# A transformer block in fp32 on one core: attention scores of two or four heads through one bank and one Exp, and other due times for projections

## The chip, the core and the metric

The kernel runs on one core of one Trainium2 chip. The metric is the device time of one execution in microseconds. PE is TensorE (the weight loads have a row of their own, PEld), DVE is VectorE, ACT is ScalarE, POOL is GpSimd, and SP is the engine that issues nearly all DMAs.

## The reference

One pre-norm transformer block over 2048 tokens of width 448: layer norm, attention with 16 heads of 28 in a sliding window of 256 tokens, a residual, layer norm, a gated GELU feed-forward of width 1792, and a residual. All in float32.

```python
def _A_ref(x, wqkv, wo):
    B, S, D = x.shape
    H = 16; Dh = D // H; W = 256
    qkv = (lambda x, *d: x.transpose(*d))((x @ wqkv).reshape(B, S, 3, H, Dh), 2, 0, 3, 1, 4)
    q, k, v = qkv[0], qkv[1], qkv[2]
    scores = jnp.einsum("bhqd,bhkd->bhqk", q, k) * (Dh ** -0.5)
    idx = jnp.arange(S)
    mask = (idx[:, None] - idx[None, :] >= 0) & (idx[:, None] - idx[None, :] < W)
    scores = jnp.where(mask[None, None], scores, -1e9)
    p = _softmax(scores, axis=-1)
    o = jnp.einsum("bhqk,bhkd->bhqd", p, v)
    return (lambda x, *d: x.transpose(*d))(o, 0, 2, 1, 3).reshape(B, S, D) @ wo
...
x = A_x
h = x + _A_ref(_layernorm(x, axis=-1), A_wqkv, A_wo)
h2 = h + _B_ref(_layernorm(h, axis=-1), B_w_gate, B_w_up, B_w_down)
```

`_B_ref` is `(gelu(x @ w_gate) * (x @ w_up)) @ w_down`.

## The kernel before, in words

**Tiling.** The 2048 tokens are 16 tiles of 128, in 4 chunks `c` of 4 tiles. The 16 heads are 4 groups `g` of 4 heads. A *block* `B = 4c + g` is the attention of one chunk for one group of heads, 16 blocks in all. To keep float32 accuracy on TensorE, an operand is kept as a high part and a low part (`to_hi` on ACT, L349; `to_lo`, the difference, mostly on DVE, L352), and a product is a sum of several matmuls (`TERMS`, 11 per projection tile).

**Stages of a chunk.** Layer norm (`ln1`), then the projections `project` to q and k (L622: 7 tiles of 11 matmuls a chunk, 128x512 each; their parts go out to DRAM through SP, L632 and L634), and `values` (L570). `loads` brings q and k back, laid out by head (`rq`, `rk`, L654).

**Stages of a block.** `scores` (L672) gives query-by-key scores, of which DVE takes the row maxima (L676). `maxima` puts the maxima, split in two parts, into extra rows of `rq` (L703 on TensorE, then two ACT copies), so that a second product of `rk` and `rq` yields key-by-query scores with the maximum already subtracted. `probs` does that second product (L744) and the Exp on ACT (L748), for each of the six key tiles `m` that a chunk's four query tiles can see. Key tile `m` has the query tiles `parts(m)`: one for m = 0 and 5, two for m = 1 and 4, three for m = 2 and 3. The first chunk has only m = 2 to 5. Before, `probs` is called once for each of the 4 heads `j`: one matmul of 128, 256 or 384 columns into a bank of its own, one Exp out of it. `select` masks the edges on POOL (L759) for all four heads together, `attend` multiplies by the values (L778) in two halves of three key tiles, `drain` transposes and divides by the sum, and after every second group `output` applies the output weights (L835) and adds to the residual `hres`.

**Feed-forward.** 56 products of a chunk and 128 of the inner columns. The first four use full-height matmuls (L1008) and are partly done while attention still runs; all later ones run as pairs of half-height matmuls (L984). Their order on TensorE is written out in `feed_forward`. Weights come from DRAM (`weight_load`) and are split (`weight_splits`).

**What sets the order.** Every operation is put into a list with its engine, a cost, a latency and a *key*, a due time. `Lists.run` then goes through a model of the engines: at each step an engine takes, among the operations that could start first (within an ease of some hundredths of a microsecond), the one with the smallest key. The resulting order is the order of each engine's instructions. So a key or a cost changes the order of instructions, and all engines then run their queues in that order, waiting for one another by semaphores. The 8 banks of TensorE's output are handed out in that pass too: `allowed` gives banks 2 and 3 to `prob` (and 7 once the projections are issued), 0 and 1 to `score`, 4 and 5 to the attention sums, 6 and 7 to projections, values and outputs.

**Names that the change touches.** `EDGE` is how far ahead of a block the projections are due (`base`, L618), `LN1` and `LN2` are due times of layer norms, `LEAD` that of the second layer norm of the last two chunks against the feed-forward, `VKEY` that of the values, `FETCH` that of a DRAM-to-DRAM copy of the third weights (L896). A block is 16 units of key long. `WKEY` in the changed kernel replaces the expression `16 * NB + 5 * loaded` with `NB = 16` and `loaded` 0 and 1.

Of the kernel before, what the change touches and what calls it, by code (L numbers as in the profile page):

```python
# [11 lines left out]
AF = mybir.ActivationFunctionType  # L12
# [9 lines left out]
SCALE = float(DH) ** -0.5  # L22
# [5 lines left out]
NB = NG * CS  # L28
# [4 lines left out]


LAG_T = 6
LAG_P = 15
LAG_V = 12
EDGE = 9
WIN = 14
FFN = 1000  # L40
LEAD = 30
MARGIN = 0.7
START = 0.8
EARLY = 2
# [1 line left out]
HOLDO = 1  # L46
AHEAD = 7
BEHIND = 5
LN1 = (0, -19, 55, 134)
LN2 = (166, 224)  # L50
VKEY = (-30, -23, 14, 24)
VHALF = 0
FETCH = 170
PKS = 3
POOLED = (3,)
PKX = (2, 3)
# [12 lines left out]
def mm(n):  # L69
    return max(n / 2400 + 0.0155, 0.115)  # L70
# [156 lines left out]
def block_kernel(ctx: ExitStack, tc, x, wqk_in, wv_in, wo_in, ffn_in, out):  # L227
    nc = tc.nc
# [332 lines left out]
               [WVRAW(p, b), WV(p, 0, b)], [WV(p, 1, b)], port=True)  # L561

    def values(t, p, n):
        key = 64 * (t // 4) + VKEY[t % 4] if t > 3 else 8 * t - 37 if not p else VHALF + 6 * t
        b = Bank("v")
        w = slice(224 * p, 224 * (p + n))
        c = slice(128 * col(t), 128 * col(t) + 128)
        for a in range(NP):
            h, wb, xb = TERMS[a]
            op("pe", mm(224 * n), 0.29 if n == 1 else 0.38, key + a / 16, lambda a=a, h=h, wb=wb, xb=xb: nc.tensor.matmul(  # L570
                bank[b.k][:, 0:224 * n], xT[:, xb, c], wv[:, h, wb, w], start=(a == 0),
                stop=(a == NP - 1)), [XT(col(t)), *(WV(p + i, h, wb) for i in range(n))], () if a else [V(t, p, n)], b, tag="v")
        op("act", 0.29 if n == 1 else 0.47, 0.39 if n == 1 else 0.57, key + 1, lambda: to_hi(
            v[:, at_v(t), 8 * p:8 * (p + n), 0:DH], bank[b.k][:, 0:224 * n].rearrange("p (h d) -> p h d", d=DH)),
           ["ones"], [V(t, p, n)], b)
# [35 lines left out]
    def project_tile(c, m):  # L611
        g, s = divmod(m, 2)
        cc = 12 * (c % 2)
        hl, both, tok = pk_at()
        B = 4 * c + g
        b = Bank("proj")
        per = 1 if m == 6 else 2
        base = 16 * B - EDGE  # L618
        for a in range(NP):
            h, wb, xb = TERMS[a]  # L620
            key = -33 + 6 * m + a / 4 if B < 2 else base - WIN * (1 - (s * NP + a) / (per * NP))
            op("pe", mm(512) + 0.002, 0.403, key, lambda a=a, h=h, wb=wb, xb=xb: nc.tensor.matmul(  # L622
                bank[b.k], wqk[m][:, h, wb, :], xT[:, xb, cc * 128:cc * 128 + 512], start=(a == 0),
                stop=(a == NP - 1)), [span("xT", cc, 4), WQK(m, h)], (), b, tag="proj")
# [106 lines left out]
    def pp_at(o, n, j=None):  # L731
        return [span("pp", 4 * (o + i) + (j or 0), 4 if j is None else 1) for i in range(n)]

    ORDER = {0: 0, 1: 1.3, 2: 4, 3: 8, 4: 12, 5: 14.6}

    def probs(B, m, j, o):
        u = B % 2
        lo, hi = parts(m)
        n = (hi - lo + 1) * 128
        b = Bank("prob")  # L740
        key = 16 * B + LAG_P + ORDER[m] + j * n / 384

        def one():
            nc.tensor.matmul(bank[b.k][:, 0:n], rk[u][0:104, j, m * 128:m * 128 + 128],  # L744
                             rq[u][0:104, j, lo * 128:(hi + 1) * 128], start=True, stop=True)

        def exp():
            nc.scalar.activation(pp[:, j, o * 128:o * 128 + n], bank[b.k][:, 0:n], AF.Exp, scale=SCALE)  # L748
        q = [("rk", u, m), *(("pick", u, j) for j in range(4)), *((w, u, i) for i in range(lo, hi + 1) for w in ("rq", "rx"))]
        op("pe", mm(n), 0.19 + n / 2400, key, one, q, (), b, tag="prob")  # L750
        op("act", 0.065 + n * 0.00088, 0.16 + n * 0.00088, key, exp, (), pp_at(o, hi - lo + 1, j), b, tag="exp")

    def select(B, m, o):
        lo, hi = parts(m)
# [177 lines left out]
    def feed_forward():  # L932
        first = [4 * sum(GROUPS[:gi]) + k for gi, gn in enumerate(GROUPS) for k in range(gn)]
        loaded = split = -1
        n = 0
        for gi, gn in enumerate(GROUPS):
            for c in range(4):
                down = [Bank(("down", i)) for i in range(4)]
                for k in range(gn):
                    i = sum(GROUPS[:gi]) + k  # L940
                    while loaded < 2:
                        loaded += 1
                        split += 1
                        weights(loaded, 16 * NB + 5 * loaded if loaded < 2 else FFN + 30 * first[loaded] - 20)
                    if n == PAIRED:
                        for cc in (1, 2, 3, 0):
                            cs = slice(512 * cc, 512 * cc + 512)
                            dma(FFN + 30 * PAIRED - 25 + cc, 128, lambda cs=cs: nc.sync.dma_start(
                                f(rec[2][64:128, cs]), f(xT[0:64, 3, cs])), [span("xT", 4 * cc, 4), "fp"], [("xh", cc)])
                    product(n, i, c, k, gn, gi, down)  # L950
                    while split < NF - 1 and first[split + 1] <= n + BEHIND:
                        split += 1
                        weight_splits(split, FFN + 30 * first[split] - 20, phase[n][0][0:1])
                    while loaded < NF - 1 and first[loaded + 1] <= n + AHEAD:
                        loaded += 1
# [168 lines left out]
    for c in range(CS):  # L1124
        project(c)
        if c == 0:
            clear()
            for t in range(4):
                values(t, 1, 1)
        else:  # L1130
            values(4 * c + 2, 0, 2)
            values(4 * c + 3, 0, 2)
        if c == 3:
            free("wqkfree", ["proj"])
            free("wvfree", ["v"])
            ln2(0)
        for g in range(NG):
            B = 4 * c + g
            loads(B)
            if B in (1, 2):  # L1140
                wo_weights(2 * B - 2)
                wo_weights(2 * B - 1)
            for i in range(4):
                for j in range(4):
                    scores(B, i, j)
                if i % 2:
                    maxima(B, i // 2)
            at = slots(B)
            for half in ((0, 1, 2), (3, 4, 5)) if c else ((2, 3), (4, 5)):
                for m in half:  # L1150
                    for j in range(4):
                        probs(B, m, j, at[m])
                    select(B, m, at[m])
                attend(B, half, at)
            drain(B)
            if g % 2:
                output(g // 2, c)
            if g == 0 and c < 3:
                ln1(c + 1)
# [106 lines left out]
```

## Time and profile before

| | |
|---|---|
| time, median of 3 runs | 727.81 us (727.71 to 727.92) |
| time of the profiled execution | 727.88 us |
| its span | 726.2 us |
| instructions | 15085 |
| DMA | 82.06 MB, mean 113 GB/s |

Times in the profile count from the start of the span. A row of a group has the line, the engine, the operation, output and inputs with their shapes, the count, then busy time in us and the mean of one in ns, and last the idle time of the engine just before these instructions and what ended it. A matmul's end in the profile is modelled, so how fast TensorE goes is read from the starts of matmuls that follow each other.

### The profile page before, as it was taken

The numbers are of one execution on the slowest core, as the hardware profiler recorded it, in microseconds if no ns is written. First come the engines' busy times: TensorE is split into PE (matmuls) and PEld (weight loads), VectorE is DVE, ScalarE is ACT, GpSimd is POOL, SyncE is SP. The second block draws the span as 40 slices with busy tenths as digits, with TensorE's granted clock in tenths as the row PEclk, the third lists the DMA queues.
The fourth block names the chain that finished last, engine by engine and source line by source line (L and its number), as shares of the span: only waits on it lengthen the run. The fifth ranks groups of instructions, "written<-read, shape, count | busy, mean of one in ns | idle before, by whom it ended". The sixth has DMA issues, their size and how long they took to land.

```text
span 726.2 us, 15085 instructions
## 1 busy us (share of the span) xinstructions
PE 717.8 (99%) x5732; PEld 594.4 (82%) x5732; DVE 401.4 (55%) x1067; ACT 366.4 (50%) x927; POOL 162.6 (22%) x285
## 2 busy tenths in 40 slices
PE   8999999999999999999999999999999999999997
PEld 7887778878787877778888888888888888888886
DVE  7968779978787769658464313244133234232224
ACT  7738777777867787786453222244222223222221
POOL 5504743544354446741000000000000000000000
PEclk9999999999999999999999999999999999999999
DMA  8896867888548984342732000012100000001002
GB/s 308 268 311 211 234 159 203 214 255 207 161 122 241 242 234 136 77 112 42 203 105 84 1 2 1 1 44 83 42 1 2 1 1 1 2 1 51 19 34 102
DMA packets 96929, 82.06 MB, mean 113 GB/s; under 512 B 41736, under 2 KB 83016, under 8 KB 96840
## 3 DMA queue, kind: packets, MB, share of 16 engines
q1 hardware_dynamic: 96712, 80.98, 38.5%
q8 instruction: 45, 0.74, 0.4%
q14 instruction: 28, 0.23, 0.1%
q10 hardware_dynamic: 144, 0.11, 0.0%
HBM read 50.27 MB, written 31.03 MB: 112 GB/s over the span
## 4 chain that ended last, share of the span: by engine, by line
PE 94%; DVE 2%; ACT 1%; issue 1%; DMA 1%; POOL 0%; SPq 0%; DVEq 0%; POOLq 0%
PE bank L984 53%; PE bank L622 10%; PE bank L744 6%; PE bank L672 6%; PE bank L778 5%; PE bank L570 5%; PE bank L835 5%; PE bank L1008 3%; DMA hres<-in_x_dram 1%; PE bank L404 1%; DVE mt L676 1%; PE bank L703 0%; ACT pp L748 0%; DVE hres L1086 0%; ACT xT L349 0%
## 5 line engine op out<-in xcount | busy, mean ns | idle before, releaser
L676 DVE CUSTOM_DVE_ANT_0 mt<-bank,mt 128x384 bf16<-128x384 f32 (+2 forms) x256 | 126.8, 526 | 29.0 <-PE bank L672 27.2
L748 ACT ACTIVATE pp<-bank 128x384 f32<-128x384 f32 (+2 forms) x352 | 122.5, 388 | 39.8 <-PE bank L744 36.8
L1050 DVE TENSOR_TENSOR mt<-bank,mt 128x512 f32<-128x512 f32 x54 | 37.1, 688 | 143.3 <-ACT mt L1048 143.3
L759 POOL TENSOR_SCALAR_AFFINE_SELECT pp<-pp 128x512 f32<-128x512 f32 x120 | 75.9, 646 | 107.6 <-ACT pp L748 86.3
L744 PE MATMUL bank<-rq,rk 104*128 104x384 f32 (+2 forms) x352 | 97.6, 303 | 0.6 <-ACT pp L748 0.2
L622 PE MATMUL bank<-xT 128*128 128x512 f32 x308 | 94.9, 400 | 0.0
L1048 ACT ACTIVATE mt<-bank 128x512 f32<-128x512 f32 x54 | 32.2, 596 | 118.0 <-PE bank L984 118.0
L984 PE MATMUL bank<-xT,rk 64*128 64x512 f32 x656 | 82.0, 388 | 0.0
L984 PE MATMUL bank<-xT,rec 64*128 64x512 f32 x656 | 81.9, 388 | 0.0
L672 PE MATMUL bank<-rk,rq 84*128 84x384 f32 (+2 forms) x256 | 80.8, 346 | 0.8 <-DVE mx L676 0.5
L744 PEld LDWEIGHTS bank<-rq,rk 104*128 104x128 f32 x352 | 65.0, 189 | 17.4 <-ACT pp L748 5.9
L984 PEld LDWEIGHTS bank<-xT,rk 64*128 64x128 f32 x656 | 63.0, 184 | 12.2
L984 PEld LDWEIGHTS bank<-xT,rec 64*128 64x128 f32 x656 | 63.0, 184 | 12.1
L1086 DVE TENSOR_TENSOR hres<-bank,hres 128x448 f32<-128x448 f32 (+1 forms) x65 | 35.7, 611 | 66.9 <-PE bank L984 64.8
L990 ACT ACTIVATE e<-bank 1x1 f32<-1x1 f32 x162 | 25.7, 158 | 81.2 <-PE bank L984 80.5
L984 PE MATMUL bank<-xT,proj 64*128 64x512 f32 x533 | 66.6, 388 | 0.0
L622 PEld LDWEIGHTS bank<-xT 128*128 128x128 f32 x308 | 55.4, 189 | 7.4 <-ACT v L349 0.4
L984 PEld LDWEIGHTS bank<-xT,proj 64*128 64x128 f32 x533 | 51.1, 184 | 9.9
L672 PEld LDWEIGHTS bank<-rk,rq 84*128 84x128 f32 x256 | 46.3, 189 | 12.2 <-DVE mx L676 5.2
L570 PE MATMUL bank<-proj,xT 128*128 128x448 f32 (+1 forms) x220 | 51.0, 337 | 0.2 <-ACT v L349 0.2
L778 PE MATMUL bank<-pp,v 128*29 128x384 f32 (+2 forms) x704 | 45.4, 388 | 0.0
L349 ACT ACTIVATE rq<-bank 8x512 fp32r<-8x512 f32 x64 | 37.5, 586 | 13.6 <-PE bank L703 12.6
(147 smaller groups left out, 1088.5 us busy)
## 6 DMA issues: line engine op xcount, KB each, us to landing
rk<-k SPq DMA_DIRECT2D x44, 336.0 KB
rq<-q SPq DMA_DIRECT2D x32, 336.0 KB
v<-in_ffn_dram SPq DMA_DIRECT2D x7, 736.0 KB
q<-proj SPq DMA_DIRECT2D x11, 448.0 KB
raw<-in_ffn_dram SPq DMA_DIRECT2D x6, 736.0 KB
xn<-xn SPq DMA_DIRECT2D x72, 56.0 KB
xT<-xn SPq DMA_DIRECT2D x20, 192.0 KB
hres<-in_x_dram SPq DMA_DIRECT2D x16, 224.0 KB
```

The costliest lines, as they stand in the source:

```text
L349: nc.scalar.activation(dst, src, AF.Copy)
L570: op("pe", mm(224 * n), 0.29 if n == 1 else 0.38, key + a / 16, lambda a=a, h=h, wb=wb, xb=xb: nc.tensor.matmul(bank[b.k][:, 0:224 * n], x ...
L622: op("pe", mm(512) + 0.002, 0.403, key, lambda a=a, h=h, wb=wb, xb=xb: nc.tensor.matmul(bank[b.k], wqk[m][:, h, wb, :], xT[:, xb, cc * 128 ...
L672: nc.tensor.matmul(bank[b.k][:, o:384], rq[u][0:3 * DH, j, i * 128:i * 128 + 128], rk[u][0:3 * DH, j, m0 * 128:(i + 3) * 128], start=True, ...
L676: nc.vector.tensor_tensor_reduce(junk[s % 2][:, o:384], bank[b.k][:, o:384], mask[:, o:384], 1.0, -BIG, OP.add, OP.max, mx[i // 2][:, i % ...
L744: nc.tensor.matmul(bank[b.k][:, 0:n], rk[u][0:104, j, m * 128:m * 128 + 128], rq[u][0:104, j, lo * 128:(hi + 1) * 128], start=True, stop=True)
L748: nc.scalar.activation(pp[:, j, o * 128:o * 128 + n], bank[b.k][:, 0:n], AF.Exp, scale=SCALE)
L759: nc.gpsimd.affine_select(a, a, pattern=[[0, 4], [-cm, 128]], compare_op=op_, fill=0.0, base=0, channel_multiplier=cm)
L778: nc.tensor.matmul(bank[b.k][32 * j:32 * j + DH + 1, lo * 128:(hi + 1) * 128], v[:, at_v(4 * c - 2 + m), 4 * g + j, :], pp[:, j, at[m] * 1 ...
L835: op("pe", mm(D), 0.38, wk, lambda a=a, h=h, oh=oh, wh=wh, i=i, k=k: nc.tensor.matmul(bank[k.k][:, 0:D], ohl[:, h, oh, i * 128:(i + 1) * 1 ...
L984: nc.tensor.matmul(bank[bk.k][:, 0:n], w, m, start=bool(start), stop=bool(stop), tile_position=(64 * x, 0), skip_group_check=True)
L1050: op("dve", 0.605, 0.702, key + 2 * NP, lambda: nc.vector.tensor_tensor(blocks(g2), src(1), blocks(g2), op=OP.mult), [*G2, *held[1]], G2, ...
```

## The change

`probs` is called once for a key tile instead of once for each head. It puts `G = 512 // n` heads into one bank: four heads where a key tile has one query tile (n = 128), two where it has two (n = 256), one where it has three (n = 384). One Exp then reads the whole bank and writes `G` strided pieces. The planner's cost for the matmuls is a new formula. The due times named above get other values; for the last chunk the projections are due 4 units earlier (`ELAST`), and its second value tile 2 units earlier (`VLAST`).

```diff
+VLAST = (-30, -25, 14, 24)
+ELAST = 4
+WKEY = (256, 261)
...
-EDGE = 9
+EDGE = 8
...
-LEAD = 30
+LEAD = 10
...
-LN1 = (0, -19, 55, 134)
-LN2 = (166, 224)
+LN1 = (0, -19, 55, 128)
+LN2 = (166, 231)
...
-FETCH = 170
+FETCH = 210
...
-        key = 64 * (t // 4) + VKEY[t % 4] if t > 3 else 8 * t - 37 if not p else VHALF + 6 * t
+        key = 64 * (t // 4) + (VKEY if t < 12 else VLAST)[t % 4] if t > 3 else 8 * t - 37 if not p else VHALF + 6 * t
...
-        base = 16 * B - EDGE
+        base = 16 * B - EDGE - (ELAST if c == 3 else 0)
...
-    def probs(B, m, j, o):
+    def probs(B, m, o):
         u = B % 2
         lo, hi = parts(m)
         n = (hi - lo + 1) * 128
-        b = Bank("prob")
-        key = 16 * B + LAG_P + ORDER[m] + j * n / 384
-
-        def one():
-            nc.tensor.matmul(bank[b.k][:, 0:n], rk[u][0:104, j, m * 128:m * 128 + 128],
-                             rq[u][0:104, j, lo * 128:(hi + 1) * 128], start=True, stop=True)
-
-        def exp():
-            nc.scalar.activation(pp[:, j, o * 128:o * 128 + n], bank[b.k][:, 0:n], AF.Exp, scale=SCALE)
...
-        op("pe", mm(n), 0.19 + n / 2400, key, one, q, (), b, tag="prob")
-        op("act", 0.065 + n * 0.00088, 0.16 + n * 0.00088, key, exp, (), pp_at(o, hi - lo + 1, j), b, tag="exp")
+        G = 512 // n
+        for j in range(0, 4, G):
+            b = Bank("prob")
+            key = 16 * B + LAG_P + ORDER[m] + j * n / 384
+
+            def some(j=j, b=b):
+                for i in range(G):
+                    nc.tensor.matmul(bank[b.k][:, n * i:n * i + n], rk[u][0:104, j + i, m * 128:m * 128 + 128],
+                                     rq[u][0:104, j + i, lo * 128:(hi + 1) * 128], start=True, stop=True)
+
+            def exp(j=j, b=b):
+                nc.scalar.activation(pp[:, j:j + G, o * 128:o * 128 + n],
+                                     bank[b.k][:, 0:G * n].rearrange("p (g t) -> p g t", g=G), AF.Exp, scale=SCALE)
...
+            cost = G * (n / 2400 + 0.009)
+            op("pe", cost, cost + 0.17, key, some, q, (), b, tag="prob")
+            op("act", 0.065 + G * n * 0.00088, 0.16 + G * n * 0.00088, key, exp, (),
+               [p for i in range(G) for p in pp_at(o, hi - lo + 1, j + i)], b, tag="exp")
...
-                        weights(loaded, 16 * NB + 5 * loaded if loaded < 2 else FFN + 30 * first[loaded] - 20)
+                        weights(loaded, WKEY[loaded] if loaded < 2 else FFN + 30 * first[loaded] - 20)
...
-                    for j in range(4):
-                        probs(B, m, j, at[m])
+                    probs(B, m, at[m])
```

The planner's cost of one matmul, `mm(n)`, is `max(n / 2400 + 0.0155, 0.115)` us; it stays in use for all other matmuls.

More of the change, by code (lines that the diff above doesn't have):

```diff
@@ L739, in probs @@
         n = (hi - lo + 1) * 128
-        b = Bank("prob")
-        key = 16 * B + LAG_P + ORDER[m] + j * n / 384
-        def one():
-            nc.tensor.matmul(bank[b.k][:, 0:n], rk[u][0:104, j, m * 128:m * 128 + 128],
-                             rq[u][0:104, j, lo * 128:(hi + 1) * 128], start=True, stop=True)
-        def exp():
-            nc.scalar.activation(pp[:, j, o * 128:o * 128 + n], bank[b.k][:, 0:n], AF.Exp, scale=SCALE)
-        q = [("rk", u, m), *(("pick", u, j) for j in range(4)), *((w, u, i) for i in range(lo, hi + 1) for w in ("rq", "rx"))]
-        op("pe", mm(n), 0.19 + n / 2400, key, one, q, (), b, tag="prob")
-        op("act", 0.065 + n * 0.00088, 0.16 + n * 0.00088, key, exp, (), pp_at(o, hi - lo + 1, j), b, tag="exp")
+        G = 512 // n
[9 more added lines that the diff above has]
+                                     bank[b.k][:, 0:G * n].rearrange("p (g t) -> p g t", g=G), AF.Exp, scale=SCALE)
+            q = [("rk", u, m), *(("pick", u, i) for i in range(4)),
+                 *((w, u, i) for i in range(lo, hi + 1) for w in ("rq", "rx"))]
+            cost = G * (n / 2400 + 0.009)
+            op("pe", cost, cost + 0.17, key, some, q, (), b, tag="prob")
+            op("act", 0.065 + G * n * 0.00088, 0.16 + G * n * 0.00088, key, exp, (),
+               [p for i in range(G) for p in pp_at(o, hi - lo + 1, j + i)], b, tag="exp")
     def select(B, m, o):
```

## The prediction

> **What bounds the kernel now.** I read the page first (shares of busy time, then the chain that ended last), then the busy time by stretch, then the single matmuls in order of time, and last what TensorE's weight loads waited for.
>
> ```profile
> PE 717.8 (99%) x5732; PEld 594.4 (82%) x5732; DVE 401.4 (55%) x1067; ACT 366.4 (50%) x927; POOL 162.6 (22%) x285
> ...
> PE 94%; DVE 2%; ACT 1%; issue 1%; DMA 1%; POOL 0%; SPq 0%; DVEq 0%; POOLq 0%
> ```
>
> TensorE is busy for 717.8 of 726.2 us and is 94% of the chain that ended last. But a busy row is not yet a row at its peak, so I look at the stretches:
>
> ```profile
> 60.00:255.00 195.00, 194.68 (x1354) 154.77 (x1353) 157.74 (x527) 149.03 (x374) 94.21 (x156) 1.00 0.75 207
> 255.00:322.00 67.00, 65.51 (x458) 48.42 (x457) 49.37 (x156) 55.40 (x148) 41.62 (x64) 1.00 0.50 134
> 322.00:336.00 14.00, 14.00 (x82) 11.00 (x80) 11.28 (x23) 9.18 (x18) 0.23 (x1) 1.00 0.25 74
> 336.00:720.00 384.00, 384.00 (x3507) 328.65 (x3507) 133.36 (x221) 113.32 (x318) 3.26 (x8) 1.00 0.12 37
> ```
>
> The columns are the length, then busy time of PE, weight load, DVE, ACT and POOL, then the granted clock. From 336 us on the feed-forward part runs with PE full, and DVE and ACT at about a third. The diff leaves its matmuls alone, and in the built order of the two programs they are the same, so I take those 384 us as fixed. Attention lies between 40 and 322 us; there DVE is busy 81% (157.74 of 195) and ACT 76% (149.03 of 195). In the stretch 255 to 322 the weight loads are busy only 72% (48.42 of 67) against 79% before it: PE runs thinner there although its row says 65.51 of 67. The clock is 1.00 throughout, so it is no part of the question.
>
> How fast PE can go is read from the starts of matmuls that follow each other:
>
> ```profile
> 152.20 0.39 PE L622 MATMUL bank<-xT 128*128 128x512 f32 x1
> 152.43 0.28 PE L744 MATMUL bank<-rq,rk 104*128 104x256 f32 x1
> 152.55 0.40 PE L622 MATMUL bank<-xT 128*128 128x512 f32 x1
> ...
> 164.66 0.22 PE L744 MATMUL bank<-rq,rk 104*128 104x128 f32 x1
> 164.72 0.45 PE L622 MATMUL bank<-xT 128*128 128x512 f32 x1
> ```
> ```profile
> 183.62 0.34 PE L744 MATMUL bank<-rq,rk 104*128 104x128 f32 x2
> 183.80 0.68 PE L622 MATMUL bank<-xT 128*128 128x512 f32 x2
> ```
> ```profile
> 304.43 0.45 PE L744 MATMUL bank<-rq,rk 104*128 104x128 f32 x3
> 304.71 0.69 PE L1008 MATMUL bank<-xT,proj 128*128 128x512 f32 x2
> ```
> ```profile
> 28.00 2.45 PE bank L570 x22
> ```
>
> A 512-column matmul takes 0.23 us of PE (152.20 to 152.43), a 256-column one 0.12, a lone 128-column one 0.06 (164.66 to 164.72). But two 128-column ones in a row take 0.18, three 0.28: every one after the first costs about 0.11, because the next weights are not in yet. The 22 matmuls of 224 columns say the same, 2.45/22 = 0.11 each although 224 columns would stream in less than the 0.12 of 256. So 0.11 us is what one weight load paces.
>
> **The change part by part.** The matmuls of the two built programs are the same in number and shape (352 of the scores for Exp, and all others). Nothing is taken from PE; only order, waits and Exps change. I sum against the profiled execution, 727.88 us (its span 726.2 and 1.68 around it), 0.07 over the median of 727.81.
>
> *Runs of four (added).* Where a key tile has one query tile, the four heads' 128-column matmuls are now issued together: 28 runs of four (16 last tiles and 12 first tiles). By the rows above a run of four takes 0.06 + 3 x 0.11 = 0.39 instead of 4 x 0.06 = 0.24. In the built order 23 of the 112 stood right behind another before, 85 do after: 62 more at 0.05 each, **+3.1 us**. All of it lies on PE, so on the path. Bounds: 0 (if the successors hide it) and 28 x 0.15 = 4.2. Runs of two with 256 columns cost nothing: 0.12 covers the 0.11 of a load. The Trainium skill, "TensorE: Matmul & The Clock Gate", section "Back-to-back issue gap", gives about 81 ns per matmul for a sustained stream with 128 columns; by it, as an estimate, a run of four would take 0.32 and this term would be 1.9 us smaller (28 x 0.07). The three-in-a-row at 304.43 stands against it: its second and third cost 0.11 each.
>
> *Exps and waits (removed).* The page by shape:
>
> ```profile
> L748 ACT ACTIVATE pp<-bank 128x256 f32<-128x256 f32 x112 | 39.5, 382 | 13.9 <-PE bank L744 12.8
> L748 ACT ACTIVATE pp<-bank 128x128 f32<-128x128 f32 x112 | 27.9, 278 | 16.8 <-PE bank L744 15.5
> ...
> L1048 ACT ACTIVATE mt<-bank 128x512 f32<-128x512 f32 x54 | 32.2, 596 | 118.0 <-PE bank L984 118.0
> ```
>
> 112 Exps of 278 ns become 28 of 512 columns, 112 of 382 ns become 56. For a 512-column Exp I take the 596 ns of the other 512-column activation: 31.1 + 42.8 us of ACT become 16.7 + 33.4, 23.8 us less. ACT is not the bound, so this by itself is worth nothing. What it buys is waits of PE for a bank that Exp has not left yet:
>
> ```profile
> L744 PE MATMUL bank<-rq,rk x352: 221/285/448, 53.4 to 320.8; 104*128 104x384 f32 x64, 104*128 104x256 f32 x56, 104*128 104x128 f32 x56
> its engine sat idle before it (us, times) until:
>   ACT pp L748: 6.1, 23
>   issue: 1.4, 7
>   ACT rq L349: 1.3, 6
>   ACT xn L399: 1.3, 2
>   ACT proj L349: 0.6, 1
>   ACT xT L349: 0.6, 1
> ```
>
> TensorE sat 11.3 us before these 352 matmuls, in 40 waits. In the built order 341 of them carry a wait now and 199 after. If a wait is late as often and as long as now, 199/341 of 11.3 remain, 6.6: **-4.7 us**. Bounds: 0 (each group waits as long as its parts did together) and -7.2, which is 224/352 of 11.3, all that the two regrouped shapes have. I take the count, because the slack in the order is not smaller than now (rival 1).
>
> *Projections of the last chunk, and the constants.* "4 slots sooner" moves keys, not places: since attention's own keys are met sooner, in the built order the projection matmuls (L622) stand later. Between the first Exp scores of block 4 and of block 8 there are 87 of them before and 45 after; between 8 and 12, 59 and 81; behind the first ones of block 12, 0 and 18. They are the work that PE does while it would wait for DVE and ACT. Where they are missing now:
>
> ```profile
> L744 PEld LDWEIGHTS bank<-rq,rk 104*128 104x128 f32 x93 | 16.9, 188 | 5.0 <-ACT pp L748 1.9 <-ACT xT L349 0.6 <-ACT rq L349 0.6
> L672 PEld LDWEIGHTS bank<-rk,rq 84*128 84x128 f32 x49 | 8.8, 188 | 4.8 <-DVE mx L676 3.6 <-DVE hres L838 0.2 <-issue 0.2
> ```
> ```profile
> L744 PEld LDWEIGHTS bank<-rq,rk 104*128 104x128 f32 x85 | 15.9, 189 | 3.4 <-ACT pp L748 0.8 <-ACT xn L399 0.6 <-issue 0.4
> L672 PEld LDWEIGHTS bank<-rk,rq 84*128 84x128 f32 x55 | 9.7, 190 | 2.0 <-DVE xn L441 0.6 <-DVE mhl L696 0.3 <-issue 0.2
> ```
>
> The first pair is from 255 to 320 us, the second from 120 to 185, the same length: 9.8 us of idle before these loads against 5.4, so the last chunk loses 4.4 us more. Eighteen matmuls (18 x 0.23 = 4.1 us of cover) now stand in block 12. I take half of the 4.4, **-2.2 us**, since blocks 13 to 15 get no more cover than before; bounds 0 and -4.4. The middle gives cover away, 42 matmuls in blocks 4 to 7; there 45 are left, about 11 a block, where blocks 13 to 15 have none, and I put it at 0; its bound is the same 4.4, upward.
>
> *Moved at no cost.* The later projections push their stores and the q and k loads of the last blocks down SP's queue; in the built order all four loads of the last block stand ahead of the second weight fetch (now two of them stand behind it), and between the last projection and the last block's first scores PE still has most of blocks 13 and 14 to do. The transfer of the third weights (FETCH) keeps its place among the loads of block 13 in SP's queue; LEAD and the two layer-norm keys reorder ACT and DVE work that feeds products past 336 us, where both engines are two thirds idle. If that cover were gone, each late tile would show as one PE gap of a transfer's length in the 384 us; I see none coming. WKEY writes the old values (256 and 261) in another form.
>
> Sum: 727.9 + 3.1 - 4.7 - 2.2 = **724.1 us**.
>
> **The rivals.**
>
> 1. *Bank held too long; slower.* A bank now serves 512 columns: after the last matmul's start come the matmul's own 0.31 (306 ns, the mean below), Exp's 0.60 and a weight load of 0.19 before it can be used again, 1.10 us. Adding up the spacings above along the built order, at least 1.10 and in the middle 1.3 us of PE work stand between the uses that follow closely; slack 0.2.
>
> ```profile
> L744 PE MATMUL bank<-rq,rk 104*128 104x256 f32 x112 | 32.5, 306 | 0.1
> ```
>
> For the 128-column form of now the same sum is 0.22 + 0.28 + 0.19 = 0.69, the order holds 0.74 in the middle, a slack of 0.05, and PE still waited in only 40 cases; that speaks against it. For it: an ACT instruction of half a microsecond in front of Exp uses up 0.2. If half of the 84 groups are late by today's mean (11.3/40 = 0.28), they cost 11.8, and with the other 115 waits at today's rate (3.8) it is 15.6 instead of 11.3: 727.9 + 3.1 + 4.3 - 2.2 = 733.1. It decides from about 24 late groups on: 24 x 0.28 + 3.8 + 3.1 - 2.2 = 11.4, the waits of now.
>
> 2. *The middle runs dry; no change.* Blocks 4 to 7 without 42 projections wait for DVE as the last chunk does now: +4.4 on the sum, 728.5. For it: DVE is at 81% there, and the blocks come closer together. Against: the projections' evacuations leave DVE and ACT with them.
>
> 3. *ACT's relief reaches further.* All waits of the two shapes go (-7.2) and all of the last chunk's excess (-4.4): 727.9 + 3.1 - 11.6 = 719.4. For it: 23.8 us less on an engine that was 76% busy. Against: the largest single releaser of L672 in the last chunk is DVE, which gets no relief.
>
> **How the numbers follow.** Forecast 0.62, rival 1 0.14, rival 2 0.14, rival 3 0.10. A measurement of this kernel tells about 0.2% from no change, 1.5 us. The forecast's own range, by its terms' bounds taken half way, is 721 to 727, so it counts 0.60 as faster and 0.02 as same; rival 3 is faster; rival 2 is same with 0.12 and slower with 0.02; rival 1 is slower with 0.13 and same with 0.01. Faster 0.70, same 0.15, slower 0.15. For 8 in 10 the range goes from 720.0, close to rival 3, to 729.5, past rival 2; rival 1 stays outside.
>
> **What would show it.** Right: 352 score matmuls, 212 Exps, the 512-column ones near 596 ns; in a run of four, starts 0.06, 0.11, 0.11, 0.11 apart; idle before their loads near 6 to 7 us instead of 11.3; ACT near 343 us busy; the feed-forward stretch still 384 us, beginning near 332 instead of 336. Wrong: more idle before these loads than 11.3 us (rival 1); idle before the weight loads of L672 in the middle grown to the last chunk's (rival 2); or a PE gap behind 336 us.

## The result, and the profile after

The changed kernel takes **725.56 us**, the median of 8 runs (724.81 to 726.36). The kernel before, beside it, takes 727.77 (8 runs, 727.48 to 727.92). The ratio is 0.9969 with a 95% interval of 0.9959 to 0.9980: faster by 0.3%. The profiled execution took 724.81 us with a span of 723.1, against 727.88 and 726.2 before. So the profiled executions differ by 3.07 us and the medians by 2.2; the profile says where the first lies, and the experiments on the clock say part of why the median keeps less.

The page of the kernel after, busy time by engine and the shares of the chain that ended last:

```profile
PE 713.5 (99%) x5732; PEld 593.2 (82%) x5732; DVE 399.2 (55%) x1067; ACT 354.8 (49%) x787; POOL 162.7 (23%) x285
...
PE 94%; ACT 3%; DMA 1%; issue 1%; DVE 1%; POOL 0%; SPq 0%; DVEq 0%; ACTq 0%
```

TensorE issues as many matmuls as before, 140 activations are gone, and TensorE is still 94% of the chain. The stretches of the kernel after, in the columns of the prediction:

```profile
60.00:255.00 195.00, 194.38 (x1378) 155.39 (x1377) 156.16 (x529) 143.50 (x281) 96.69 (x157) 1.00 0.77 205
255.00:322.00 67.00, 65.53 (x461) 49.00 (x462) 51.51 (x160) 52.36 (x107) 39.86 (x61) 1.00 0.56 152
322.00:336.00 14.00, 14.00 (x83) 12.02 (x84) 11.72 (x27) 7.89 (x16) 2.10 (x6) 1.00 0.13 30
336.00:720.00 384.00, 383.11 (x3489) 327.58 (x3485) 132.90 (x217) 112.34 (x315) 0.81 (x3) 1.00 0.12 36
```

More matmuls start between 60 and 255 us (1378 instead of 1354). The end of the chain of waits says what that is worth, first of the kernel before, then of the kernel after:

```profile
336.10 383.58 PE bank L984 x3504
```
```profile
332.57 3.88 PE bank L995 x36
336.64 379.97 PE bank L995 x3468
```

The half-height pairs of the feed-forward part begin 3.53 us sooner (332.57 for 336.10) and take 384.04 us from there to the end of this chain (336.64 + 379.97 - 332.57) instead of 383.58: 0.46 is given back, most of it in one gap of TensorE at 336.1 us. Together that is the difference of 3.07.

The single matmuls in order of time, where runs of four now stand:

```profile
141.51 0.56 PE L751 MATMUL bank<-rq,rk 104*128 104x128 f32 x4
141.91 0.45 PE L625 MATMUL bank<-xT 128*128 128x512 f32 x1
```

Four 128-column matmuls hold TensorE for 0.40 us, start to start. The Exps by shape:

```profile
L755 ACT ACTIVATE pp<-bank 128x384 f32<-128x384 f32 x128 | 58.1, 491 | 17.1 <-PE bank L751 14.6 <-POOL oblk L820 0.6 <-ACT pp L755 0.3
L755 ACT ACTIVATE pp<-bank 128x512 f32<-128x512 f32 x84 | 47.7, 598 | 21.9 <-PE bank L751 13.5 <-PE bank L789 6.7 <-POOL ohl L355 0.4
```

All 212 are there, the 512-column ones at 598 ns. What TensorE waited for before the score matmuls of Exp in the kernel after:

```profile
its engine sat idle before it (us, times) until:
  ACT pp L755: 4.8, 14
  ACT rq L352: 4.2, 11
  issue: 0.2, 1
```

9.2 us in 26 waits, for 11.3 in 40 before. Of the scores for the maxima, the largest releaser, before and after:

```profile
  DVE mx L676: 5.7, 14
```
```profile
  DVE mx L679: 2.2, 8
```

And the weight loads by the time that TensorE sat idle before them, in the last chunk (255 to 320 us), then in the middle (120 to 185):

```profile
L751 PEld LDWEIGHTS bank<-rq,rk 104*128 104x128 f32 x88 | 14.3, 189 | 3.8 <-ACT rq L352 1.4 <-ACT pp L755 1.0
L1019 PEld LDWEIGHTS bank<-xT,proj 128*128 128x128 f32 x57 | 10.1, 189 | 2.6 <-ACT v L1044 1.3 <-issue 0.2
L675 PEld LDWEIGHTS bank<-rk,rq 84*128 84x128 f32 x48 | 8.7, 189 | 3.7 <-DVE mx L679 1.4 <-issue 0.8 <-DVE rcp L824 0.6
```
```profile
L751 PEld LDWEIGHTS bank<-rq,rk 104*128 104x128 f32 x97 | 16.9, 190 | 2.4 <-ACT rq L352 0.6 <-ACT pp L755 0.5
L675 PEld LDWEIGHTS bank<-rk,rq 84*128 84x128 f32 x65 | 12.0, 189 | 3.3 <-DVE bnmv L386 0.6 <-DVE mhl L699 0.6 <-DVE oT L828 0.6
```

The two kinds of scores lose 7.5 us in the last chunk (9.8 before) and 5.7 in the middle (5.4 before). But the early feed-forward products there (L1019) lose 2.6, half of it to one wait for an ACT copy; before (L1008) they lost 0.8. The three lines together lose 10.1 us in the last chunk, for 10.6 before.

### The profile page after: what moved, and what is told of

Its sections match the earlier page's. It is cut to its first block, busy times and chain, and to the rows that moved or that the text cites. A ratio compares the mean times of both kernels' runs of the same rounds, so it can differ in the third digit from the quotient of the medians.

```text
span 723.1 us, 14945 instructions
## 1 busy us (share of the span) xinstructions
PE 713.5 (99%) x5732; PEld 593.2 (82%) x5732; DVE 399.2 (55%) x1067; ACT 354.8 (49%) x787; POOL 162.7 (23%) x285
## 4 chain that ended last, share of the span: by engine, by line
PE 94%; ACT 3%; DMA 1%; issue 1%; DVE 1%; POOL 0%; SPq 0%; DVEq 0%; ACTq 0%
PE bank L995 53%; PE bank L625 9%; PE bank L751 7%; PE bank L675 6%; PE bank L789 5%; PE bank L846 5%; PE bank L573 5%; PE bank L1019 3%; DMA k<-pp 1%; ACT pp L755 1%; PE bank L407 1%; ACT rq L352 1%; ACT xT L352 0%; DMA hres<-in_x_dram 0%; PE bank L706 0%
## 5 line engine op out<-in xcount | busy, mean ns | idle before, releaser
L679 DVE CUSTOM_DVE_ANT_0 mt<-bank,mt 128x384 bf16<-128x384 f32 (+2 forms) x256 | 127.5, 526 | 31.6 <-PE bank L675 29.8
L755 ACT ACTIVATE pp<-bank 128x384 f32<-128x384 f32 (+1 forms) x212 | 105.7, 533 | 39.0 <-PE bank L751 28.2
L625 PE MATMUL bank<-xT 128*128 128x512 f32 x308 | 96.5, 399 | 0.2 <-ACT pp L755 0.2
L751 PE MATMUL bank<-rq,rk 104*128 104x384 f32 (+2 forms) x352 | 82.1, 306 | 1.0 <-ACT pp L755 0.5
L751 PEld LDWEIGHTS bank<-rq,rk 104*128 104x128 f32 x352 | 59.7, 190 | 13.6 <-ACT pp L755 4.3
```

What stands on the lines that cost most here:

```text
L679: nc.vector.tensor_tensor_reduce(junk[s % 2][:, o:384], bank[b.k][:, o:384], mask[:, o:384], 1.0, -BIG, OP.add, OP.max, mx[i // 2][:, i % ...
L751: nc.tensor.matmul(bank[b.k][:, n * i:n * i + n], rk[u][0:104, j + i, m * 128:m * 128 + 128], rq[u][0:104, j + i, lo * 128:(hi + 1) * 128] ...
L755: nc.scalar.activation(pp[:, j:j + G, o * 128:o * 128 + n], bank[b.k][:, 0:G * n].rearrange("p (g t) -> p g t", g=G), AF.Exp, scale=SCALE)
```

## The experiments

Each was compared with the kernel before on the same chip (medians of 727.64 to 727.86). "Clock" is the mean granted clock of a run.

### One part without the other

**Grouping alone** (e1): the kernel after with every due time as before.

```diff
-EDGE = 8
+EDGE = 9
-ELAST = 4
+ELAST = 0
-VLAST = (-30, -25, 14, 24)
+VLAST = VK0 = (-30, -23, 14, 24)
-LEAD = 10
+LEAD = 30
-LN1 = (0, -19, 55, 128)
+LN1 = (0, -19, 55, 134)
-LN2 = (166, 231)
+LN2 = (166, 224)
-FETCH = 210
+FETCH = 170
```

> The regrouped scores and Exps alone, with all due times of the kernel before (727.8). In the built order 23 projection matmuls stand behind block 12's first Exp scores (0 before, 18 in the changed kernel) and 201 score matmuls carry a wait. Theory A (the gain comes from the grouping: fewer waits, ACT relief that lets projections stand later): 725 to 726.5, nearly the changed kernel's 725.6. Theory B (the gain comes from the new due times of the last chunk): 727.5 or more, since the runs of four add 3.1 us.

Measured: 729.15 us (728.86 to 730.49, 10 runs), ratio 1.0022 [1.0013, 1.0031]: slower than before by 1.5 us. Its chain and its waits of the scores for the maxima:

```profile
340.60 379.89 PE bank L995 x3468
```
```profile
  DVE mx L679: 6.1, 16
```

The same last 3468 pairs begin 3.96 us later than in the kernel after. That is what theory B expected of the grouping alone; its other half, that the due times make the gain, fails in e2 below. The waits before the score matmuls of Exp are as low as in the kernel after (8.6 us in 25), so the grouping brings those. What it doesn't bring is the other kind: the wait for DVE's maxima stays at 6.1 us where the kernel after has 2.2. And the projections already stand late here: in the built order 93 of their matmuls come behind the first Exp scores of block 8 and 23 behind those of block 12, for 99 and 18 in the kernel after and 59 and none before.

**Due times alone** (e2): the kernel before with the new values, one Exp per head.

```diff
-EDGE = 9
+EDGE = 8
+VLAST = (-30, -25, 14, 24)
+ELAST = 4
-LEAD = 30
+LEAD = 10
-LN1 = (0, -19, 55, 134)
-LN2 = (166, 224)
+LN1 = (0, -19, 55, 128)
+LN2 = (166, 231)
-FETCH = 170
+FETCH = 210
-        base = 16 * B - EDGE
+        base = 16 * B - EDGE - (ELAST if c == 3 else 0)
```

(and the one line of `values` that uses `VLAST`)

> The new due times alone, scores and Exps by head as before. In the built order no projection stands behind block 12's first Exp scores, as before. Theory A: no gain, 727 to 729. Theory B: about 725.5 or less, since the runs of four are not paid.

Measured: 740.28 us (4 runs), ratio 1.0174 [1.0160, 1.0188]: 12.6 us slower, which neither theory expected. The stretches around its worst place:

```profile
293.45:296.86 3.41, 2.58 (x12) 1.73 (x11) 3.13 (x14) 3.27 (x10) 3.08 (x7) 1.00 0.79 202
296.86:310.51 13.65, 13.60 (x73) 9.81 (x76) 8.45 (x31) 8.38 (x21) 6.58 (x14) 0.50 0.38 88
```

For 13.65 us the granted clock is 0.50, worth 6.8 us at full clock. Without the grouping the projections stay early: 55 of their matmuls come behind the first Exp scores of block 8, none behind those of block 12. So the two parts don't add: +1.5 and +12.6 apart, -2.2 together.

**The price in the planner alone** (e4): the kernel before, ungrouped, with the new formula for the matmul's cost.

```diff
-        op("pe", mm(n), 0.19 + n / 2400, key, one, q, (), b, tag="prob")
+        op("pe", n / 2400 + 0.009, n / 2400 + 0.179, key, one, q, (), b, tag="prob")
```

> The kernel before with one edit: the planner's price of an Exp score matmul is n / 2400 + 0.009 us as in the changed kernel, not at least 0.115. Nothing is grouped. Theory A (grouping makes the gain): no gain, 727 to 729; in the built order no projection stands behind block 12's first Exp scores. Rival E (the truer price makes the gain, by placing the projections later): 725.5 to 726.5.

Measured: 734.62 us (733.32 to 735.79, 4 runs), ratio 1.0093 [1.0079, 1.0107], again outside both expectations. Nothing is different but the order, and it costs 7 us (5.7 in the one run with the full clock); 48 projection matmuls come behind the first Exp scores of block 8, none behind those of block 12. So neither the price nor the due times move the projections back by themselves; the grouping (with its price, e1) does.

**Single due times** of the kernel after: `ELAST` (e8) and the second layer norm of chunk 1 (e11), whose work falls into the attention of the last chunk.

```diff
-ELAST = 4
+ELAST = 0
```

> The changed kernel without the 4 units by which the last chunk's projections are due sooner (ELAST 0); all other due times are the new ones. In the built order 25 projection matmuls stand behind block 12's first Exp scores instead of 18. If those 4 units decide the difference between the grouping alone (729.15) and the changed kernel (725.56): 728 to 729.5. If the other due times do: within 0.7 of 725.6.

Measured: 725.79 us (725.46 to 727.44, 7 runs), ratio 0.9975 [0.9964, 0.9986]. The 4 units are worth 0.2 us by the medians, which these runs can't tell from nothing.

```diff
-LN2 = (166, 231)
+LN2 = (166, 224)
```

> The changed kernel with LN2's second value back at 224: the second layer norm of chunk 1 is due 7 units sooner, away from the thin stretch at 283 us where its splits stand on ACT. Of the new due times LEAD, FETCH and LN1 leave every queue of the changed kernel in the same order (the built orders agree to the instruction), and ELAST was worth 0.2 us, so what separates the grouping alone (729.15) from the changed kernel (725.56) is EDGE, VLAST or this. If it is this one: 728 to 729.5. If not: 725 to 726.5.

Measured: 728.58 us (727.22 to 732.25, 12 runs), ratio 1.0013 [1.0000, 1.0025]: 3.0 us more than with 231. With `LEAD`, `FETCH` or the last value of `LN1` alone set back in the kernel after, the built order of every engine stays what it is, so these three do nothing here. Without the layer norm's new due time the change gains nothing (`EDGE` and `VLAST` were not run by themselves). In its profiled execution (731.93 us), a thin stretch and half the clock behind it stand again:

```profile
275.57:278.98 3.41, 1.71 (x8) 1.14 (x7) 3.35 (x7) 2.16 (x6) 3.22 (x5) 1.00 0.54 180
278.98:285.81 6.83, 6.83 (x37) 4.39 (x36) 5.79 (x21) 5.18 (x12) 3.74 (x6) 0.50 0.67 196
```

The longest gap of that stretch, on TensorE, and what DVE does meanwhile:

```profile
278.18 0.79 PE L751 MATMUL bank<-rq,rk 104*128 104x384 f32 x3 [1.54 <-DVE mx L679]
```
```profile
274.61 1.63 DVE L355 TENSOR_TENSOR xT<-xT 128x384 fp32r<-128x384 f32 x1
276.27 1.25 DVE L355 TENSOR_TENSOR xT<-xT,lasthi 64x128 fp32r<-64x128 f32 x1
```

With the old key the low parts of the layer norm's output stand on DVE in front of the maxima, for 2.9 us, and TensorE waits 1.54 us. In the kernel after two such instructions (from 278.59 us) take 0.56 and 0.61 us; why they take longer here was not followed up.

Its 12 runs fall into groups by clock: 727.2 to 727.3 at 0.999, 728.5 to 728.9 at 0.997, 729.8 to 732.3 at 0.993 and 0.994. Its runs at 0.999 are 2.1 to 2.4 us above those of the kernel after at 0.999 or more (by means and by the fastest), so the old key costs that much in order, and the rest is clock.

### What a bank shared by heads costs and saves

**Runs of four, doubled** (e9): each of their matmuls is issued twice, 112 more matmuls of 128 columns in the same order.

```diff
-                for i in range(G):
+                for i in [i for i in range(G) for _ in range(2 if G == 4 else 1)]:
```

> The changed kernel with each one-tile score matmul of a run of four issued twice, runs of eight: 112 more matmuls of 128 columns, all queues otherwise in the same order (the planner's prices are left alone). It prices the runs by themselves. If every matmul behind another costs 0.11 us and all of it lies on the path: 12.3 us over the changed kernel's 725.6, 737 to 738. If 0.06: 6.7, 732. If the waits around the runs take it up: under 730.

Measured: 736.71 us (736.02 to 737.89, 4 runs), ratio 1.0123 [1.0109, 1.0136]: 11.15 us over the kernel after, 0.10 for each, a little under the expected 737.

```profile
161.13 1.00 PE L751 MATMUL bank<-rq,rk 104*128 104x128 f32 x8
161.97 0.57 PE L675 MATMUL bank<-rk,rq 84*128 84x384 f32 x2
```

Eight take 0.84 us. Nearly all of it reaches the end, so a 128-column matmul in a run lies on the path at 0.10 us.

**Exp by head out of the shared bank** (e5): the matmuls stay grouped, the 352 Exps of before come back.

```diff
-            def exp(j=j, b=b):
-                nc.scalar.activation(pp[:, j:j + G, o * 128:o * 128 + n],
-                                     bank[b.k][:, 0:G * n].rearrange("p (g t) -> p g t", g=G), AF.Exp, scale=SCALE)
+            def exp(i, j=j, b=b):
+                nc.scalar.activation(pp[:, j + i, o * 128:o * 128 + n], bank[b.k][:, n * i:n * i + n], AF.Exp, scale=SCALE)
...
+            for i in range(G):
+                op("act", 0.065 + n * 0.00088, 0.16 + n * 0.00088, key, lambda i=i, exp=exp: exp(i), (),
+                   pp_at(o, hi - lo + 1, j + i), b, tag="exp")
```

> The changed kernel with the same banks and runs, but an Exp for each head out of the shared bank (352 Exps as before, 366 us of ACT). PE's waits stay at 195. If the fewer waits make the gain: 725.6 to 726.5, idle before the score loads about as in the changed kernel (9 us). If ACT's relief (12 us less busy) makes it: 728 to 731, since the runs of four and the longer hold of a bank are paid and nothing is gained.

Measured: 727.22 us (726.04 to 728.03, 11 runs), ratio 0.9990 [0.9981, 0.9999]. That lies between the two expected ranges. Its runs at clock 1.0 take 726.04 to 726.23, those of the kernel after 724.81 and 725.54, so without any relief of ACT the time is about 0.9 us longer where both have the full clock (1.2 by the fastest runs), and 1.7 in the medians. How much of that is ACT's relief itself isn't shown, since this kernel is planned anew with its Exps: the idle time before the score matmuls of Exp is as in the kernel after (9.6 us for 9.2), but the wait for DVE's maxima is 5.8 us, although all due times are the new ones.

**Two heads to a bank at most** (e3): runs of two instead of four.

```diff
-        G = 512 // n
+        G = min(2, 512 // n)
```

> The changed kernel with at most two heads in a bank: the 112 one-tile matmuls go in 56 runs of two instead of 28 of four, with 56 Exps of 256 columns instead of 28 of 512. A one-tile matmul right behind another: 62 instead of 85. Theory A with runs of four at 0.39 us: 23 x 0.05 = 1.2 us less for loads, against about 28 more waits of which one in ten is late by 0.3 (0.8 us) and 4.7 us more ACT work: 725 to 726, within 0.5 us of the changed kernel. If runs of four cost nothing, it is slower than the changed kernel by 0.8 or more, 726.4 and up.

Measured: 734.22 us (734.09 to 734.48, 4 runs), ratio 1.0089 [1.0075, 1.0103], far above the 725 to 726 of theory A, although its runs of 128 columns are half as long. Its single matmuls in order of time, and the stretches:

```profile
286.90 0.44 PE L751 MATMUL bank<-rq,rk 104*128 104x128 f32 x2 [1.51 <-ACT rq L352]
287.18 0.39 PE L675 MATMUL bank<-rk,rq 84*128 84x384 f32 x1
288.72 0.69 PE L751 MATMUL bank<-rq,rk 104*128 104x128 f32 x2 [1.16 <-ACT pp L755]
```
```profile
281.74:285.16 3.42, 3.30 (x35) 2.06 (x34) 3.36 (x14) 1.74 (x4) 1.23 (x2) 1.00 0.98 301
285.16:288.57 3.41, 0.89 (x4) 0.41 (x3) 3.15 (x10) 3.28 (x8) 0.00 (x0) 1.00 0.41 97
288.57:295.40 6.83, 5.39 (x33) 3.04 (x33) 3.29 (x11) 6.08 (x15) 5.98 (x10) 0.50 0.38 95
295.40:298.81 3.41, 3.41 (x21) 3.06 (x18) 3.25 (x12) 2.05 (x4) 3.24 (x5) 1.00 0.00 0
```

From 285.16 us on TensorE has 4 matmuls in 3.41 us, and then the clock is 0.50 for 6.83. This experiment can't say what runs of four cost against runs of two, because its order is thin elsewhere; it says what a thin place costs beyond itself.

### The clock

**Fillers** between the matmuls: the planner puts a transpose that nobody reads into TensorE's longer gaps, up to the planner's time `WARM`. Raised from 26 to 330 it places 50 more in e7, on the kernel of e3, and 51 more in e6, on the kernel after.

```diff
-WARM = 26.0
+WARM = 330.0
```

> The kernel with at most two heads in a bank (734.2, clock 0.995 in every run, 6.8 us at half clock from 288.6) with the same kind of fills. Theory C: clock back to 0.999, and 3.4 us of the 8.7 that it lost against the changed kernel come back, 730 to 732 with the fills' own cost. Rival D: clock stays 0.995 and the time 734 to 738.

> The changed kernel with 51 transposes of a constant tile (0.11 us each) put where the order has TensorE idle in the attention part, most of them in the last chunk. They give nothing to the output. Theory C (in some runs of the changed kernel a thin stretch near 283 us makes the chip halve TensorE's clock for 3.4 us): granted clock 0.999 to 1.0 in every run and a spread under 0.5 us, where the changed kernel had 0.997 to 1.0 and 724.8 to 726.4; the median then is 724.8 plus what of 5.6 us of fills falls on no idle, 725 to 727. Rival D (the spread has another cause, transfers for example): clocks and spread stay as they were.

Measured: e7 731.03 us (730.68 to 731.18, 5 runs), ratio 1.0044 [1.0031, 1.0056], clock 1.0 in all runs. That is 3.2 below e3, nearly the 3.4 that 6.83 us at half clock cost, although more work was issued. e6: 727.87 us (727.68 to 728.18, 11 runs), ratio 1.0001 [0.9992, 1.0010], clock 0.999 to 1.0 in all. Its spread is 0.5 us where that of the kernel after is 1.55, so the fillers take most of the spread away, but cost 2.3, more than expected.

### The one late copy

The wait of L1019 in the last chunk, in order of time in the kernel after, TensorE and then ACT:

```profile
284.13 1.35 PE L751 MATMUL bank<-rq,rk 104*128 104x128 f32 x8
286.56 0.73 PE L1019 MATMUL bank<-xT,proj 128*128 128x512 f32 x2 [1.09 <-ACT v L1044]
```
```profile
285.26 0.31 ACT L352 ACTIVATE lasthi<-xT 64x128 fp32r<-64x128 f32 x1
285.58 0.31 ACT L352 ACTIVATE xT<-xT 64x128 fp32r<-64x128 f32 x1
285.91 0.60 ACT L1044 ACTIVATE v<-bank 128x512 f32<-128x512 f32 x1
```

The copy L1044 frees the bank of an early product. It stands in ACT's queue behind the splits of the second layer norm's output. With the old key (e11) TensorE waits 1.03 us for the same copy, which there stands behind two Exps, so the wait isn't shown to come from the new key.

**The copy sooner** (e10):

```diff
-            op("act", 0.49, 0.605, 16 * NB - 20, lambda ...
+            op("act", 0.49, 0.605, 16 * NB - 60, lambda ...
```

> The changed kernel with the copies of the first feed-forward products out of their banks due 40 units earlier (the key 16 * NB - 20 becomes 16 * NB - 60). In its profile TensorE waits 1.1 us at 285.4 for such a copy, which stands on ACT behind two layer-norm splits; in the new built order the copy stands three places sooner. Theory C: no window thin enough for half clock, clock 0.999 and more in every run, 723.5 to 725. If the wait only moves to another instruction: 725.5 or more, clocks as in the changed kernel.

Measured: 726.64 us (726.26 to 727.41, 11 runs), ratio 0.9983 [0.9975, 0.9992]: 1.1 more than the kernel after, at a clock of 0.999 or more in all runs. The wait for this copy is gone, but the order is another one: L1019 waits 1.2 us for DVE (L849) instead, and TensorE waits 12.5 us before the score matmuls of Exp instead of 9.2.

**Work into the gap** (e12): the order is kept, and the one pair of 256-column matmuls of block 14 that stands before the wait is issued four times, 6 more matmuls or 0.72 us.

```diff
-                for i in range(G):
+                for i in [i for _ in range(4 if (B, m, j) == (14, 1, 2) else 1) for i in range(G)]:
```

> The changed kernel with one pair of 256-column score matmuls (block 14, key tile 1, the second pair of heads) issued four times instead of once: six more matmuls, 0.72 us of TensorE, just ahead of the 1.1 us for which it waits at 285.4 us; the same values are written again, and no queue's order changes. Theory C (a thin stretch here halves the clock in some runs): clock 0.999 or more in every run, all runs at 724.8 to 725.6, median near 725.0 where the changed kernel had 725.56 with runs up to 726.4. Rival D (the spread has another cause): clocks down to 0.997 and runs up to 726.4 as before. If the six matmuls lie on the path after all: 726.3.

Measured: **724.87 us** (724.71 to 725.74, 5 runs), ratio 0.9963 [0.9950, 0.9977], clock 0.999 to 1.0 in all runs.

```profile
284.59 2.06 PE L751 MATMUL bank<-rq,rk 104*128 104x128 f32 x14
287.03 0.73 PE L1019 MATMUL bank<-xT,proj 128*128 128x512 f32 x2 [0.37 <-ACT v L1044]
```

The gap shrinks from 1.09 to 0.37 and the median is 0.7 lower, with the best run no better (724.71 for 724.81): added work that nobody reads costs nothing that shows here. One run at clock 1.0 took 725.74, above the expected 725.6, so not all of the spread is clock. The intervals of e12 and of the kernel after overlap, so that it is the better version is likely and not settled by five runs.

## Why the prediction was right, and where its sizes were off

It said 724.1 us and faster, and 725.56 lies in its range. The profiled execution came out at 724.81, 0.7 above the sum. What bounds the kernel, the direction and the cost of the runs were right; that the sum came so close is in part luck, since its terms as measured don't add up to it. Taken from the views, the runs (+3.0 at most), the waits before Exp scores (-2.1), the scores of the last chunk (-2.3), the maxima elsewhere (-1.3), L1019 (+1.8) and the feed-forward pairs (+0.46) give -0.4 and not -3.07. What does add up is the time from each matmul's start to the next one's, until the first pair, 3.54 us less: the Exp scores hold TensorE for 53.3 us after and 53.4 before (the 128-column ones 1.7 more, the larger ones 1.9 less), and nearly all of the gain lies behind the matmuls of the output weights (36.7 us for 38.7) and of the values (38.2 for 39.7), a wait being counted to the matmul before it. Which step of the change did that stays open.

Step by step:

*What bounds the kernel.* It held: TensorE is the chain, and the pairs take 384 us wherever they begin. In e1, e8, e11 and the kernel after, the last 3466 or 3468 matmuls of them take 379.89 to 379.97 us.

*Runs of four, +3.1.* The price of a run held: 0.40 where 0.39 was worked out. By the starts of matmuls, where no wait stands behind them, the 112 take 0.101 us each after and 0.074 before, 112 x 0.027 = 3.0; with spacings above 0.15 us counted too it is 0.102 and 0.082, 2.3 in all. e9 shows that such a cost lies on the path. That the 256-column ones in runs of two take less than by themselves (1.3 us in all, waits behind them included) was not forecast. The 81 ns of the Trainium skill ("TensorE: Matmul & The Clock Gate", "Back-to-back issue gap") don't hold here: the 112 additional ones of e9 cost 0.10 each.

*Exps and waits, -4.7.* This term was mis-sized. The number of waits fell as the count of instructions that carry one (40 to 26, where the ratio of the forecast gives 23), but each got longer: 9.2/26 = 0.35 us instead of 0.28. Idle time fell by 2.1 us in this view. What remains isn't only a bank that Exp still holds: nearly half (4.2 us) now waits for `rq`, the copy of the maxima on ACT, for which 1.3 stood before. Waits for the one input took the place of waits for the other.

*The last chunk, -2.2.* The size came out for the two kinds of scores, 9.8 to 7.5, but with L1019 the idle time fell by 0.5 only (10.6 to 10.1), so that this agreement is luck; and the cause was only half right. Half right: the prediction put the later projections down to "attention's own keys", and e1, e2 and e4 show that it is the grouping that moves them (behind block 8's first Exp scores 93 with it alone, 55 and 48 without it). Missing: the second layer norm's key was costed at nothing with the cover "past 336 us, where both engines are two thirds idle". Its ACT splits run at 285 us instead, and the copy behind them keeps TensorE 1.09 us (with the old key the same wait is there, 1.03); the loads of L1019 lose 2.6 us, 0.8 before, where the forecast had no term. The same key is what the change gains most from: with the old one its DVE splits stand in front of the maxima (e11), for which there was no term either.

*A wait without a term.* The wait for DVE's maxima (L679) fell from 5.7 to 2.2 us, 3.5 in all. In the last chunk it went from 3.6 to 1.4, which is in the term above; the other 1.3 was not forecast. Little of it is saved: all idle time before these matmuls went from 9.2 to 8.8 us, since waits for other DVE instructions took its place (4.6 us for 2.3). In e1, with the old due times, the wait for the maxima stays at 6.1, in e5, with the new ones, at 5.8, and in e11, with the old key of `LN2` alone, it is 2.2, so it is a matter of the whole order and not of one due time, nor of DVE's load, which is nearly the same (399.2 us busy for 401.4).

*ACT.* It is busy 354.8 us, not 343. The Exps take 105.7 us for 122.5 (these are the page's rows for this line), 16.8 less and not 23.8, because the forecast multiplied means, and in the profile of before consecutive small Exps overlap. By their own rows the other activations take the same time as before (265.1 us for 265.4); ACT's busy time fell by 11.6 us only because fewer instructions overlap now (all rows add up to 22.9 us more than the busy time before, and to 16.1 more after).

*The rivals.* Bank held too long: refuted, there is less idle before these loads than before, not more. The middle dry: its sign was idle time before L672's loads in the middle as in the last chunk (4.8); it rose from 2.0 to 3.3, half way, but both kinds together lose 5.7 us there for 5.4, and 1378 matmuls started in 195 us where 1354 did, so it didn't decide. ACT's relief reaches further: no, the time is far from 719.4, and without the relief (e5) it is 0.9 to 1.7 us longer.

*What would be wrong: a gap behind 336 us.* There is one, 0.4 us in the first pairs, the "0.46 given back" above. It is a wait for a small ACT instruction, and no transfer.

*From the profile to the median.* The prediction took the clock for no part of the question, since it was 1.00 throughout. It is one after the change: the runs at a clock of 0.999 or more take 724.81 to 725.58, those at 0.997 and 0.998 take 725.69 to 726.36. Without the three runs at the lower clock the median is 725.09, so the clock accounts for some 0.5 of the 0.75 between the profiled execution and the median; the rest is spread at full clock, whose cause isn't shown.

## What to carry to other kernels

Where a planner orders the work, a change of shape, a price and a due time are one change: the grouping with its price cost 1.5 us, the price alone 7 and the due times alone 12.6, and together they saved 2.2, so none of them can be judged by itself, and a moved step has to be followed on every engine's queue (here a layer norm's splits in front of the maxima on DVE). Fewer waits don't make the waiting less in proportion, since the next input is then the late one; and idle time that is gone in one view can stand in another, so a gain is only placed when the account adds up. And where TensorE runs thin for a few microseconds, work that nobody reads can cost no more than the gap.

## What the runs showed of the hardware that was not expected

**TensorE's clock can halve after a stretch that is thin, not empty.** In e2, e3, e5 and e11 the granted clock fell to 0.50 for 3.41, 6.83 or 13.65 us, whole multiples of 3.41. Four of the five falls came behind a stretch of 3.41 us with little work; the longest gaps in it were 1.51 and 1.16 us in e3, 1.54 in e11, 0.49 in e2 and 0.48 in e5. First e5, then the fifth fall (the second of e11), whose stretch before has no gap and more work, then the kernel after, whose profiled execution kept the clock:

```profile
296.87:300.28 3.41, 2.57 (x20) 1.57 (x13) 3.21 (x10) 3.34 (x9) 3.41 (x5) 1.00 0.00 0
300.28:303.69 3.41, 3.41 (x14) 3.02 (x14) 1.09 (x4) 2.88 (x13) 2.79 (x4) 0.50 0.29 49
303.69:307.10 3.41, 3.41 (x23) 2.54 (x26) 0.66 (x2) 2.83 (x7) 2.44 (x4) 1.00 0.37 95
```
```profile
302.88:306.29 3.41, 3.32 (x18) 2.43 (x18) 3.41 (x14) 3.18 (x7) 1.70 (x4) 1.00 0.39 68
306.29:309.70 3.41, 3.41 (x10) 3.02 (x10) 2.19 (x6) 2.87 (x7) 2.23 (x3) 0.50 0.45 109
```
```profile
282.98:286.39 3.41, 2.50 (x14) 1.69 (x12) 3.10 (x10) 3.26 (x8) 2.99 (x6) 1.00 0.98 262
```

Within a profile the edges lie on one grid of 3.41 us, and the stretch of the kernel after is taken on its grid. From profile to profile the grid lies elsewhere against the program: the first edge is at 5.26 us in e3 and at 7.86 in the kernel before. Whether a thin place fills one window would then be chance, which fits that the same kernel e11 took 727.2 to 732.3 us at clocks of 0.999 to 0.993, and that with e6's fillers the spread was 0.5 us; no two profiles of one kernel show it. It isn't the only cause of spread: e10 and e12 spread by 1.15 and 1.03 us at full clock. The Trainium skill ("TensorE: Matmul & The Clock Gate", "What's actually happening") gives a free-running activity window of 3413 ns with two clocks, 4/8 and 8/8; the grid and the 0.50 agree. Its advice of no idle gaps over about 3 us ("Why this matters for your kernels") is too wide for these runs, in which gaps of 1.5 us and less were enough. What decides stays open: weight loads busy for 0.41, 1.14, 1.57, 1.73 and 2.43 us of the window were followed by half clock, while 1.69 in the kernel after was not, so that measure doesn't separate them.
